# Banded attention with fitted blocks, ahead of a ReLU-squared expert

## The chip, the cores and the metric

The kernel runs on one core of a Trainium2 chip. A core has a matrix engine (TensorE, PE in the profile, with its weight loads as PEld), a vector engine (VectorE, DVE), a scalar engine (ScalarE, ACT), a general engine (GpSimd, POOL) and a queue engine (SyncE, SP). They run side by side, each with a queue of its own, and wait for each other through semaphores. Transfers between the large memory (DRAM) and the on-chip memory (SBUF) are issued from SP or POOL and done by 16 DMA engines. TensorE writes only to PSUM, a small memory of eight banks, which VectorE and ScalarE empty. The metric is device time in microseconds (us), the median of several runs; lower is better.

## The reference, cut to what matters

Eight sequences (B) of 576 tokens (S) with eight heads (H) of 64 numbers (D). Heads 0 to 3 are sliding: a token sees itself and the 31 tokens before it. Heads 4 to 7 are dilated: a token sees those of the last 128 tokens whose distance is a multiple of 4. The attention output of all heads, 4608 tokens by 512, goes through an expert with a squared ReLU between two matrices of 512x2048 and 2048x512. Inputs and output are FP32.

```python
scores = scale * np.matmul(q, k.transpose(0, 1, 3, 2))
rel = pos[:, None] - pos[None, :]
mask_plain = (rel >= 0) & (rel < window)
mask_dil = (rel >= 0) & (rel < window * dilation) & (rel % dilation == 0)
...
attn = np.exp(scores)
attn = attn / (np.sum(attn, axis=-1, keepdims=True) + 1e-09)
return np.matmul(attn, v).astype(np.float32)
...
h = x @ w_in
r = np.maximum(h, 0.0)
g = r * r
return (g @ w_out).astype(np.float32)
```

## The kernel before

Attention goes sequence by sequence (the code calls it b, a batch), the expert token chunk by token chunk: nine chunks of 512 tokens.

`emit_loads` fetches q, k and v of a batch with 15 DMAs from POOL's queue, one for each tensor and each of five blocks of up to 128 tokens (four of 128 and one of 64). The DMA casts FP32 to FP16 on its way, in runs of one head of one token (64 numbers). nq, nk and nv have two buffers each; batches 0 and 1 are loaded at the start, then the expert's weights wi and wo (`emit_w_loads`), then batch b+2 after batch b.

`emit_transposes` (L188) turns q and k, two heads at a time, so that the head dimension lies across partitions: 40 TensorE transposes for a batch, copied out of PSUM by VectorE (L195) into QT and KT. `emit_scores` (L212) computes, for every head and each block of 128 keys, the scores against 256 queries, the block's own 128 and the next 128: 40 matmuls for a batch. The two heads of a pair use partitions 0 to 63 and 64 to 127. ScalarE takes the exponential (L224 to L226) into AT, and VectorE multiplies it by the head's mask (L228), 1280 columns a head. The dilated heads are computed like the sliding ones, with three quarters of the band masked away. `emit_av` (L241 to L250) multiplies AT by v, which carries a column of ones so that the row sums come with it; the products of a query block from its own and the previous key block are added in PSUM. VectorE normalizes (L256, L257), TensorE transposes the result (L266), and VectorE copies it to xT (L273), the expert's input.

`moe_gen` is the expert for one chunk, a generator: 64 matmuls ph (L117), relu on ScalarE (L127), square on VectorE into g (L128), then 64 matmuls po (L133), a copy to SBUF on VectorE (L143) and a store from SP (L144). It yields after about every two matmuls. `pump(n)` takes n steps of it; the attention code calls it between its own instructions, so that expert matmuls of an earlier chunk stand among attention instructions. A chunk is handed to `pump` once the batch that completes its tokens has been emitted. Tile, the framework, orders the instructions by their place in the program and by a model of when each is ready, and places the semaphores; that order is fixed when the kernel is built.

PSUM is divided into four banks for transposes and scores (ppool), two for products and transposes of the result (pbool) and two for the expert (pmool).

Of the kernel before, what the change touches and what calls it, by code (L numbers as in the profile page):

```python
# [13 lines left out]
P = 128  # L15
# [3 lines left out]
def kernel(  # L19
# [16 lines left out]
    assert DM == H * D and NTOK == B * S and D == 64  # L36
    NKC = (S + P - 1) // P
    SPAD_K = NKC * P
    SPAD_Q = (NKC - 1) * P + 256
    HP = H // 2  # L40
# [3 lines left out]
    s_chunk = [min(P, S - kc * P) for kc in range(NKC)]  # L44
    TOKC = 512
    NTOKC = NTOK // TOKC

    const = ctx.enter_context(tc.tile_pool(name="const", bufs=1))
    wpool = ctx.enter_context(tc.tile_pool(name="wpool", bufs=1))
    xtp = ctx.enter_context(tc.tile_pool(name="xtp", bufs=1))  # L50
    natp = ctx.enter_context(tc.tile_pool(name="natp", bufs=2))
    qtp = ctx.enter_context(tc.tile_pool(name="qtp", bufs=2))
    atp = ctx.enter_context(tc.tile_pool(name="atp", bufs=9))
# [3 lines left out]
    ppool = ctx.enter_context(tc.tile_pool(name="ppool", bufs=4, space=bass.MemoryType.PSUM))  # L57
    pbool = ctx.enter_context(tc.tile_pool(name="pbool", bufs=2, space=bass.MemoryType.PSUM))
    pmool = ctx.enter_context(tc.tile_pool(name="pmool", bufs=2, space=bass.MemoryType.PSUM))

    ident = const.tile([P, P], FP16, name="ident")
    make_identity(nc, ident)

    xT = xtp.tile([P, NDM, NTOK], FP16, name="xT")

    reli = const.tile([P, 256], I16, name="reli")
    nc.gpsimd.iota(reli, pattern=[[1, 256]], base=0, channel_multiplier=-1)
    relf = const.tile([P, 256], FP32, name="relf")
    nc.vector.tensor_copy(relf, reli)
    lo = const.tile([P, 256], FP16, name="lo")  # L70
    nc.vector.tensor_scalar(out=lo, in0=relf, scalar1=-0.5, scalar2=None, op0=ALU.is_gt)
    masks = {}
    for kind, dil in (("plain", 1), ("dil", DIL)):
        m5 = const.tile([P, NKC, 256], FP16, name=f"mask5_{kind}")
        hi = const.tile([P, 256], FP16, name=f"hi_{kind}")
        nc.vector.tensor_scalar(
            out=hi, in0=relf, scalar1=(W - 1) * dil + 0.5, scalar2=None, op0=ALU.is_lt
        )
        nc.vector.tensor_mul(m5[:, 0, :], lo, hi)
        if dil != 1:  # L80
            md = const.tile([P, 256], I16, name="md")
            nc.vector.tensor_scalar(
                out=md, in0=reli, scalar1=dil - 1, scalar2=None, op0=ALU.bitwise_and
            )
            mdf = const.tile([P, 256], FP16, name="mdf")
            nc.vector.tensor_scalar(
                out=mdf, in0=md, scalar1=0.5, scalar2=None, op0=ALU.is_lt
            )
            nc.vector.tensor_mul(m5[:, 0, :], m5[:, 0, :], mdf)
        for kc in range(1, NKC):  # L90
            nc.vector.tensor_copy(m5[:, kc, :], m5[:, 0, :])
        masks[kind] = m5

    wi = wpool.tile([P, NDM, DFF], FP16, name="wi")
    wo = wpool.tile([P, NFF, DM], FP16, name="wo")

    def emit_w_loads():
        for j in range(4):
# [5 lines left out]
            )  # L104
            nc.gpsimd.dma_start(
# [4 lines left out]
            )  # L110

    def moe_gen(c):
        g = gp.tile([P, NFF, TOKC], FP16, name=f"g{c}", tag="g")
        for ffc in range(NFF):
            ph = pmool.tile([P, TOKC], FP32, name=f"ph{c}_{ffc}", tag="pm")
            for dmk in range(NDM):
                nc.tensor.matmul(  # L117
                    ph,
                    wi[:, dmk, ffc * P : ffc * P + P],
                    xT[:, dmk, c * TOKC : (c + 1) * TOKC],  # L120
                    start=(dmk == 0),
                    stop=(dmk == NDM - 1),
                )
                if dmk % 2 == 1:
                    yield
# [4 lines left out]
        for t in range(TOKC // P):  # L130
            po = pmool.tile([P, DM], FP32, name=f"po{c}_{t}", tag="pm")
            for ffc in range(NFF):
# [7 lines left out]
                if ffc % 2 == 1:  # L140
                    yield
            ot = osb.tile([P, DM], FP32, name=f"ot{c}_{t}", tag="ot")
            nc.vector.tensor_copy(out=ot, in_=po)  # L143
# [7 lines left out]
    def pump(n):  # L151
        for _ in range(n):
            if not pending:
                return
            try:
                next(pending[0])
            except StopIteration:
                pending.pop(0)

    def emit_loads(b):  # L160
        nq = natp.tile([P, NKC, H, D], FP16, name=f"nq{b}", tag="nq")
        nk = natp.tile([P, NKC, H, D], FP16, name=f"nk{b}", tag="nk")
        nv = natp.tile([P, NKC, H, D + 2], FP16, name=f"nv{b}", tag="nv")
        for src, dst, isv in ((q, nq, False), (k, nk, False), (v, nv, True)):
            for kc in range(NKC):
                n = s_chunk[kc]
                d_ap = dst[0:n, kc, :, 0:D] if isv else dst[0:n, kc, :, :]
                nc.gpsimd.dma_start(  # L168
                    out=d_ap,
                    in_=src[b, :, kc * P : kc * P + n, :].transpose([1, 0, 2]),  # L170
                )
        nc.vector.memset(nv[:, :, :, D : D + 1], 1.0)
        nt = s_chunk[NKC - 1]
        if nt < P:
            nc.vector.memset(nv[nt:, NKC - 1, :, 0:D], 0.0)
        return nq, nk, nv

    def emit_transposes(b, nq, nk):
        QT = qtp.tile([P, HP, SPAD_Q], FP16, name=f"QT{b}", tag="QT")
        KT = qtp.tile([P, HP, SPAD_K], FP16, name=f"KT{b}", tag="KT")  # L180
# [148 lines left out]
```

The softmax here doesn't subtract the row's maximum and nothing guards it: scores larger than these inputs give would overflow.

## Time and profile before

| What | Value |
|---|---|
| Median of three runs | 396.25 us (395.68 to 396.54) |
| Span of the profiled execution, first to last instruction | 392.9 us |
| The profiled execution's own device time | not given apart from its span; the runs' median is 3.35 us above the span |
| Mean granted TensorE clock | 0.996 |
| Matmuls of the expert (L117, L133) | 1152 of 512 columns |
| Transposes of q and k (L188), scores (L212) | 320 and 320 |
| Products with v (L241, L246, L250), transposes of the result (L266) | 576 and 160 |
| Relu L127, square L128, mask product L228 | 600, 423 and about 820 ns each |
| Loads issued by POOL | 120 for q, k, v and 8 for weights, 0.88 to 0.99 us each on POOL |
| Bytes moved by DMA | 28.21 MB in 121950 packets, 113216 of them under 512 B |

The share of busy time is an average over the whole span. What sets the time at a place is read from the chain of waits, which follows the work that ended last back to what released it, and from the timeline of one engine, where the distance from one start to the next tells what an instruction costs when the engine is full. The time of a single matmul in the table of groups (381 ns for 512 columns) is longer than that distance, because matmuls are pipelined.

### The profile page before, as it was taken

Reading aid. Unit: us, or ns where it says so; the run is one execution under the profiler, and the core shown is the slowest. Engines: PE = TensorE matmul, PEld = TensorE weight load, DVE = VectorE, ACT = ScalarE, POOL = GpSimd, SP = SyncE. Lnnn points to the kernel's source line nnn. Section 1 sums busy time; section 2 is a strip of 40 time slices with the busy share of each in tenths; the row PEclk is TensorE's granted clock in tenths of the full one; section 3 lists DMA queues with packets and bytes.
Section 4 is the critical chain, followed back from the end, with each engine's and each line's share of the span. In section 5 each row is a group of like instructions: output and inputs, shape, how many; then the busy total and the mean of one; then the engine's idle time right before and its main releaser. Section 6 shows DMA issues by size and latency. Waiting matters only on the chain.

```text
span 392.9 us, 6401 instructions
## 1 busy us (share of the span) xinstructions
PE 377.2 (96%) x2528; PEld 170.9 (43%) x2528; DVE 221.9 (56%) x557; ACT 172.3 (44%) x337; POOL 107.6 (27%) x135
## 2 busy tenths in 40 slices
PE   1999999999999999999999999999999999999996
PEld 0445443544336433643355434642364335444442
DVE  6567544675457545775568445864576456632431
ACT  1361565136541675057523672157424851530610
POOL 9995369084003900092005610040000000000000
PEclk9999999989999999999999999999999999999999
DMA  9999999799013931199019981090110011002002
GB/s 83 143 139 188 206 163 168 114 85 97 2 55 71 141 25 53 55 109 73 29 67 75 73 76 53 28 63 0 55 53 2 0 55 53 2 28 77 5 27 82
DMA packets 121950, 28.21 MB, mean 72 GB/s; under 512 B 113216, under 2 KB 117312, under 8 KB 121920
## 3 DMA queue, kind: packets, MB, share of 16 engines
q0 software_dynamic: 116736, 18.36, 63.4%
q1 hardware_dynamic: 5184, 9.44, 6.3%
q8 instruction: 20, 0.33, 0.3%
q14 instruction: 10, 0.08, 0.1%
HBM read 36.70 MB, written 9.44 MB: 117 GB/s over the span
## 4 chain that ended last, share of the span: by engine, by line
PE 95%; POOL 1%; DMA 1%; DVE 1%; ACT 1%; issue 0%; POOLq 0%
PE po L133 34%; PE ph L117 34%; PE ps L212 10%; PE pt L188 7%; PE px L266 3%; PE pav L246 3%; PE pav L250 2%; POOL nq L168 1%; DMA nk<-in_k_dram 1%; PE pav L241 1%; ACT AT L225 0%; DVE ot L143 0%; ACT AT L226 0%; DVE xT L273 0%; ACT AT L224 0%
## 5 line engine op out<-in xcount | busy, mean ns | idle before, releaser
L133 PE MATMUL po<-wo,g 128*128 128x512 f16 x576 | 143.1, 381 | 0.0
L117 PE MATMUL ph<-xT,wi 128*128 128x512 f16 x576 | 142.4, 385 | 0.0
L127 ACT ACTIVATE rt<-ph 128x512 f16<-128x512 f32 x144 | 86.3, 600 | 108.6 <-PE ph L117 101.4
L128 DVE TENSOR_TENSOR g<-rt 128x512 f16<-128x512 f16 x144 | 60.7, 423 | 57.4 <-ACT rt L127 56.7
L117 PEld LDWEIGHTS <-wi 128*128 128x128 f16 x576 | 50.4, 98 | 51.9 <-issue 2.9
L224 ACT ACTIVATE AT<-ps 128x512 f16<-128x512 f32 x64 | 36.0, 603 | 82.3 <-PE ps L212 77.2
L133 PEld LDWEIGHTS <-g 128*128 128x128 f16 x576 | 44.8, 98 | 50.1 <-issue 3.5
L168 POOL DMA_DIRECT2D nq<-in_q_dram x40 | 33.9, 880 | 111.7 <-PE pt L188 73.1
L212 PE MATMUL ps<-QT,KT 64*128 64x256 f16 x320 | 49.0, 296 | 2.0 <-ACT AT L224 0.5
L143 DVE COPY ot<-po 128x512 f32<-128x512 f32 x36 | 24.8, 690 | 35.3 <-PE po L133 35.3
L168 POOL DMA_DIRECT2D nv<-in_v_dram x40 | 34.0, 914 | 31.9 <-PE pav L250 31.5
L225 ACT ACTIVATE AT<-ps 128x512 f16<-128x512 f32 x64 | 36.3, 603 | 10.2 <-PE ps L212 9.9
L212 PEld LDWEIGHTS <-KT 64*128 64x128 f16 x320 | 15.6, 95 | 52.8 <-issue 49.3
L228 DVE TENSOR_TENSOR AT<-AT,mask_dil 128x1280 f16<-128x1280 f16 x32 | 25.1, 820 | 21.0 <-ACT AT L226 20.9
L168 POOL DMA_DIRECT2D nk<-in_k_dram x40 | 34.3, 907 | 9.0 <-PE pt L188 3.8
L228 DVE TENSOR_TENSOR AT<-AT,mask_plain 128x1280 f16<-128x1280 f16 x32 | 25.3, 822 | 18.4 <-ACT AT L226 18.3
L257 DVE TENSOR_TENSOR x<-pav,rcp 128x256 f16<-128x256 f32 (+1 forms) x80 | 33.5, 419 | 1.4
L188 PE MATMUL pt<-ident,nq 128*128 128x128 f16 (+1 forms) x160 | 20.3, 235 | 7.7 <-DMA nq<-in_q_dram 7.6
L246 PE MATMUL pav<-nv,AT 128*128 128x65 f16 (+1 forms) x256 | 26.4, 202 | 0.9 <-DVE xT L273 0.8
L250 PE MATMUL pav<-nv,AT 128*128 128x65 f16 (+1 forms) x256 | 25.9, 200 | 0.0
L266 PE MATMUL px<-ident,x 128*128 128x128 f16 (+1 forms) x160 | 25.0, 226 | 0.4 <-DVE x L257 0.3
L226 ACT ACTIVATE AT<-ps 128x256 f16<-128x256 f32 x64 | 22.8, 404 | 1.6 <-PE ps L212 1.6
(37 smaller groups left out, 195.1 us busy)
## 6 DMA issues: line engine op xcount, KB each, us to landing
out_dram<-ot SPq DMA_DIRECT2D x36, 256.0 KB, 2.0
nq<-in_q_dram POOLq DMA_DIRECT2D x32, 128.0 KB, 4.2
nk<-in_k_dram POOLq DMA_DIRECT2D x32, 128.0 KB, 4.3
nv<-in_v_dram POOLq DMA_DIRECT2D x32, 128.0 KB, 4.5
wi<-in_moe_w_in_dram POOLq DMA_DIRECT2D x4, 512.0 KB, 13.4
wo<-in_moe_w_out_dram POOLq DMA_DIRECT2D x4, 512.0 KB, 15.2
nq<-in_q_dram POOLq DMA_DIRECT2D x8, 64.0 KB, 4.0
nk<-in_k_dram POOLq DMA_DIRECT2D x8, 64.0 KB, 3.9
```

The costliest lines, as they stand in the source:

```text
L117: nc.tensor.matmul(ph, wi[:, dmk, ffc * P : ffc * P + P], xT[:, dmk, c * TOKC : (c + 1) * TOKC], start=(dmk == 0), stop=(dmk == NDM - 1),)
L127: nc.scalar.activation(rt, ph[:], ACTF.Relu)
L128: nc.vector.tensor_mul(g[:, ffc, :], rt, rt)
L133: nc.tensor.matmul(po, g[:, ffc, t * P : (t + 1) * P], wo[:, ffc, :], start=(ffc == 0), stop=(ffc == NFF - 1),)
L168: nc.gpsimd.dma_start(out=d_ap, in_=src[b, :, kc * P : kc * P + n, :].transpose([1, 0, 2]),)
L188: nc.tensor.transpose(pt[:, kc, 0:n], src[0:n, kc, 2 * hp : 2 * hp + 2, :], ident[0:n, 0:n],)
L212: nc.tensor.matmul(o, KT[r0 : r0 + D, hp, kc * P : kc * P + P], QT[r0 : r0 + D, hp, kc * P : kc * P + 256], start=True, stop=True,)
L224: nc.scalar.activation(AT[:, 0:2, :], ps[0][:], ACTF.Exp, scale=scale)
L225: nc.scalar.activation(AT[:, 2:4, :], ps[1][:], ACTF.Exp, scale=scale)
L228: nc.vector.tensor_mul(AT[:, :, :], AT[:, :, :], m5)
L246: nc.tensor.matmul(o, AT[:, qt - 1, P : P + nq_], nv[:, qt - 1, h, 0 : D + 1], start=True, stop=False,)
L266: nc.tensor.transpose(px[:, dmc, 0:nq_], xf[0:nq_, dmc * P : dmc * P + P], ident[0:nq_, 0:nq_],)
```

## The change

The attention half is rewritten. The expert keeps its matmuls.

- *Blocks.* A sliding head is done in six blocks of 96 queries (QB) against the 128 keys that end with the block's last query; 32 pad keys stand ahead of the first (PADP). The tokens of a dilated head fall into four residue classes of 144 tokens, each of which is an ordinary sliding window of 32 in its own numbering; a class is done in two blocks of 72 queries (QD) against 128 keys, with 56 pad keys. Each product of a block with v is one matmul, with nothing added up over key blocks.
- *Counts for a batch.* 48 transposes of 96 columns for q and k (40 of up to 128 before), 24 score matmuls of 96 and 32 of 72 columns (40 of 256 before), 56 products of 65 columns (72 before), 12 transposes of 96 and 16 of 72 columns for the result (20 of up to 128 before).
- *Loads.* q and k of the sliding heads (sq, runs of 1536 bytes) and v (sv in runs of 256 bytes, sd in runs of 1024 bytes) come as FP32 from SP's queue; POOL casts them to FP16 (11 instructions a batch), and in batch 0 VectorE and ScalarE do part of it. q and k of the dilated heads (nd, runs of 3072 bytes) still come from POOL's queue with the cast in the DMA, four DMAs a batch. wi is loaded ahead of batch 0's attention, wo after it.
- *Groups.* Score matmuls stand in groups of 12 or 16, with the pump calls between the stages of a batch and none within. Every stage takes a double bank of PSUM from one pool of two (papool); the expert has four banks (pmool).
- *Buffers.* QKTp, QKTd, AT, vp, vd, sv, sd and sq have one buffer; nq and nd have two.
- *Evacuation.* The transposes of q and k are copied by VectorE and ScalarE, one each; the expert's output copy moves from VectorE to ScalarE. The exponential takes 576 columns an instruction and the mask product too.
- *Expert order.* Chunk b-1 runs among the stages of batch b, and what is left of it follows; batch 0 has no expert beside it, and chunks 7 and 8 come last. `moe_gen` has 64 steps of two matmuls (84 steps before, some without a matmul).

```diff
+    QB = 96
+    NB = S // QB
+    PADP = P - QB
+    CL = S // DIL
+    QD = CL // 2
+    PADD = P - QD
+    UW = 576
...
-    ppool = ctx.enter_context(tc.tile_pool(name="ppool", bufs=4, space=bass.MemoryType.PSUM))
-    pbool = ctx.enter_context(tc.tile_pool(name="pbool", bufs=2, space=bass.MemoryType.PSUM))
-    pmool = ctx.enter_context(tc.tile_pool(name="pmool", bufs=2, space=bass.MemoryType.PSUM))
+    papool = ctx.enter_context(tc.tile_pool(name="papool", bufs=2, space=bass.MemoryType.PSUM))
+    pmool = ctx.enter_context(tc.tile_pool(name="pmool", bufs=4, space=bass.MemoryType.PSUM))
...
+    def load_sliding_qk(b):
+        for i, src in enumerate((q, k)):
+            nc.sync.dma_start(
+                out=sq[:, i, :, :],
+                in_=src[b, 0:HH].rearrange("h (p j) d -> p h (j d)", j=6),
+            )
+
+    def load_v(b):
+        for m in range(NB):
+            lo = QB * m - PADP
+            p0 = PADP if m == 0 else 0
+            nc.sync.dma_start(
+                out=sv[p0:P, m, :, :],
+                in_=v[b, 0:HH, lo + p0 : lo + P, :].transpose([1, 0, 2]),
+            )
+        vv = v[b, HH:H].rearrange("h (i c) d -> i h (c d)", c=DIL)
+        nc.sync.dma_start(out=sd[PADD:P, 0, :, :], in_=vv[0:QD])
+        nc.sync.dma_start(out=sd[:, 1, :, :], in_=vv[QD - PADD : CL])
+
+    def load_dilated_qk(b):
+        nd = natp.tile([QB, 2, 2, 12 * D], FP16, name=f"nd{b}", tag="nd")
...
+    def cast_sliding_qk(b, engs):
+        n = natp.tile([QB, 2, 6, HH, D], FP16, name=f"nq{b}", tag="nq")
+        for i in range(2):
+            for half in range(2):
+                j0 = 3 * half
+                copy(
+                    engs[i],
+                    n[:, i, j0 : j0 + 3, :, :],
+                    sq[:, i, :, D * j0 : D * (j0 + 3)].rearrange("p h (j d) -> p j h d", d=D),
+                )
+        return n
+
+    def cast_v(engs):
+        for m in range(0, NB, 2):
+            copy(engs[0], vp[:, m : m + 2, :, 0:D], sv[:, m : m + 2, :, :])
+        for t in range(2):
+            for c in range(0, DIL, 2):
+                copy(
+                    engs[1],
+                    vd[:, t, c : c + 2, :, 0:D],
+                    sd[:, t, :, D * c : D * (c + 2)].rearrange("p h (c d) -> p c h d", d=D),
+                )
...
-            nc.vector.tensor_copy(out=ot, in_=po)
+            nc.scalar.copy(ot, po)
...
+    def t_sliding(b, n, hp):
+        pt = pa(f"pt{b}_{hp}", FP16)
+        for i in (1, 0):
+            for j in range(6):
+                nc.tensor.transpose(
+                    pt[:, i, QB * j : QB * (j + 1)],
+                    n[:, i, j, 2 * hp : 2 * hp + 2, :],
+                    ident[0:QB, 0:QB],
+                )
+        for i, eng in ((1, nc.vector), (0, nc.scalar)):
+            copy(
+                eng,
+                QKTp[:, i, hp, PADP:].rearrange("x (p j) -> x j p", j=6),
+                pt[:, i, 0:UW].rearrange("x (j p) -> x j p", p=QB),
+            )
...
+    def softmax(u, ps, mask):
+        nc.scalar.activation(AT[:, u, 0:UW], ps[:, :, 0 : UW // 2], ACTF.Exp, scale=scale)
+        nc.vector.tensor_mul(AT[:, u, 0:UW], AT[:, u, 0:UW], mask)
+
+    def s_sliding(b, hp):
+        tiles = [pa(f"ps{b}_{hp}_{half}") for half in range(2)]
+        for half, ps in enumerate(tiles):
+            for m3 in range(3):
+                m = 3 * half + m3
+                for e in range(2):
+                    r = slice(D * e, D * (e + 1))
+                    nc.tensor.matmul(
+                        ps[:, e, QB * m3 : QB * (m3 + 1)],
+                        QKTp[r, 1, hp, QB * m : QB * m + P],
+                        QKTp[r, 0, hp, PADP + QB * m : PADP + QB * (m + 1)],
+                        start=True,
+                        stop=True,
...
+    def attn(b, nq, nd, gap):
+        t_sliding(b, nq, 0)
+        pump(gap)
+        t_sliding(b, nq, 1)
+        pump(gap)
+        t_dilated(b, nd, 0)
+        pump(gap)
+        s_sliding(b, 0)
+        pump(gap)
+        t_dilated(b, nd, 1)
+        pump(gap)
+        s_sliding(b, 1)
+        pump(gap + 2)
+        s_dilated(b, 0)
+        pump(gap + 2)
+        s_dilated(b, 1)
+        pump(gap + 1)
+        xs = []
+        for mp in range(3):
+            xs.append(av_sliding(b, mp))
+            pump(gap)
+            if mp == 1:
+                x_sliding(b, 0, xs)
+                pump(gap)
...
+    nq = cast_sliding_qk(0, (nc.vector, nc.vector))
+    cast_v((nc.gpsimd, nc.scalar))
+    load_sliding_qk(1)
+    load_v(1)
+    attn(0, nq, nds[0], 0)
+    nds[1] = load_dilated_qk(1)
+    load_w_out()
     nxt = 0
...
+    for b in range(1, B):
+        pending.append(moe_gen(b - 1))
         pump(1)
+        nq = cast_sliding_qk(b, (nc.gpsimd, nc.gpsimd))
+        cast_v((nc.gpsimd, nc.gpsimd))
+        if b + 1 < B:
+            load_sliding_qk(b + 1)
+            load_v(b + 1)
+            nds[b + 1] = load_dilated_qk(b + 1)
+        attn(b, nq, nds[b], 3)
+        pump(1000)
+    for c in range(B - 1, NTOKC):
+        pending.append(moe_gen(c))
+    pump(10000)
```

The parts left out follow the same pattern: `t_dilated` has 12 transposes and four copies, `s_dilated` 16 score matmuls, `av_sliding` and `av_dilated` eight products each with a reciprocal and a multiplication on VectorE, `x_sliding` and `x_dilated` six and eight transposes with one copy on VectorE.

## The prediction

> **What bounds the kernel now.** I read the page first: busy shares, the forty slices, the chain that ended last.
>
> ```profile
> PE 377.2 (96%) x2528; PEld 170.9 (43%) x2528; DVE 221.9 (56%) x557; ACT 172.3 (44%) x337; POOL 107.6 (27%) x135
> ...
> PE   1999999999999999999999999999999999999996
> ...
> PE 95%; POOL 1%; DMA 1%; DVE 1%; ACT 1%; issue 0%; POOLq 0%
> PE po L133 34%; PE ph L117 34%; PE ps L212 10%; PE pt L188 7%; PE px L266 3%; PE pav L246 3%; PE pav L250 2%; POOL nq L168 1%; DMA nk<-in_k_dram 1%; PE pav L241 1%; ACT AT L225 0%; DVE ot L143 0%; ACT AT L226 0%; DVE xT L273 0%; ACT AT L224 0%
> ```
>
> TensorE is the chain: 68% of the span is the expert's two matmuls, about 27% attention. So removed TensorE work is removed time, provided nothing else becomes late. A busy PE isn't PE at its pace, so next I read PE's timeline in order of time (start, length, group) for start-to-start steps, first in the expert alone, then among attention work.
>
> ```profile
> 361.09 14.05 PE L117 MATMUL ph<-xT,wi 128*128 128x512 f16 x64
> 374.98 1.24 PE L133 MATMUL po<-wo,g 128*128 128x512 f16 x5
> ...
> 144.47 0.61 PE L133 MATMUL po<-wo,g 128*128 128x512 f16 x2
> 145.01 0.28 PE L212 MATMUL ps<-QT,KT 64*128 64x256 f16 x2
> 145.22 0.60 PE L133 MATMUL po<-wo,g 128*128 128x512 f16 x2
> ...
> 162.09 0.19 PE L246 MATMUL pav<-nv,AT 128*128 128x65 f16 x1
> ...
> 162.33 0.52 PE L188 MATMUL pt<-ident,nq 128*128 128x128 f16 x5
> 162.78 0.53 PE L188 MATMUL pt<-ident,nk 128*128 128x128 f16 x5
> ```
>
> 64 expert matmuls take 374.98 - 361.09 = 13.9 us, about 216 ns each (13.81 us for the 64 at 347.44 in the chain). Eight pav matmuls lie between 162.09 and 162.33: 30 ns each. Two po matmuls before a score pair take 145.01 - 144.47 = 0.54 us instead of 0.43, and the pair 0.21: going from 128-row to 64-row tiles and back costs some 0.22 us around a pair whose own streaming is 0.107. Five transposes take 0.45 us, of which four at 57 ns (two px transposes elsewhere take 0.11) and one short one explain 0.25; the fifth has 64 rows, so again 0.2 us of switching.
>
> Then the windows (length, then busy time by engine), cut at the head, the mixed middle and the end:
>
> ```profile
> 0.00:41.05 41.05, 30.99 (x221) 16.52 (x221) 26.47 (x74) 14.21 (x30) 34.65 (x48) 1.00 1.70 141
> 41.05:347.44 306.39, 304.69 (x2119) 135.78 (x2118) 182.39 (x459) 147.91 (x291) 73.00 (x88) 0.99 0.65 66
> 347.44:388.96 41.52, 41.52 (x193) 18.57 (x190) 12.31 (x25) 10.15 (x17) 0.00 (x0) 1.00 0.12 45
> ```
>
> The first ph matmul starts at 41.05 us; POOL issued descriptors for 34.65 us of that head. The middle holds 960 of the 1152 expert matmuls, 207 us, so 99 us are attention, for about 6.6 batches. From 388.96 to 392.9 is the last copy and store, 3.9 us.
>
> **What the Trainium skill says.** "TensorEngine Tiling (Array Packing)", section Key Properties: changing the tiling mode drains TensorE; the 0.11 us each way above agrees. "TensorE: Matmul & The Clock Gate", section "Wait — 56ns, not 53.3ns?": N columns take N/2.4 ns plus about 2.5. That gives 216, 56 and 30 ns for 512, 128 and 65 columns; the trace has 216, 57 and 30. "SBUF — State Buffer", section "SBUF: two separate sides": GpSimd and VectorE share a port pair as an exclusive lock, against a VectorE instruction with two SBUF inputs. No run here shows it yet: before has no GpSimd elementwise work beside L128.
>
> **The change, part by part.**
>
> *TensorE work of one batch.* Before, by those steps: 8 transpose groups x 0.455 = 3.6; 20 score pairs x 0.33 = 6.5; 72 pav x 0.030 = 2.2; transposes of x 1.0, with some 0.5 of switching for the 64-token remainder: 13.8 us. Windows of one period (131.40 to 299.00) give 12.3 to 14.4 after subtracting the expert, so the prices hold.
>
> After: 48 transposes of 96 columns (42.5 ns by the formula) = 2.0; scores 12 pairs of 96 and 16 pairs of 72 columns (32.5 ns), 1.0 if the two row halves run together, which the 0.107 above suggests, 2.1 if not; they stand in four uninterrupted groups, so four switches x 0.22 = 0.9, where before had twenty; 56 products of 65 columns x 0.030 = 1.7; 28 transposes of x, 12 x 42.5 + 16 x 32.5 ns = 1.0. All but the scores have 96, 72 or 128 rows, which I take as the 128-row mode. Sum 6.7, or 7.7 with scores one after another. I take 7.2.
>
> *New waits inside a batch.* Attention PSUM goes from 4+2 buffers to 2 double ones (papool), the expert's from 2 to 4. Each stage is followed by three pump steps, 6 matmuls x 0.216 = 1.3 us. A stage that needs both buffers (s_sliding) follows a stage evacuated by copies of 576 columns on DVE and two of 288 on ACT: the nearest row, L195, is 438 ns for 576; I allow 0.7 for the strided output, and 0.4 each for ACT (L226: 404 ns for 256). That is 0.8 to 1.0 us plus up to one relu of 600 ns ahead in ACT's queue. Behind a waiting PE instruction stand all expert matmuls, so such a wait is whole time. The exps (two of about 0.67 us, by L224's 603 for 512) have 5 pump steps, 2.2 us; the normalization before x_sliding has 1.3 against 0.2 + 0.7 plus a queued g. So 0 to 0.3 us at some six places: 0 to 2, I take 1.0 with what the casts add. A batch: 8.2 us.
>
> *Other engines per batch of about 36 us.* ACT: 16 relus 9.6, 4 output copies at about 0.6 = 2.4 (DVE's L143 was 690 ns), 8 exps 5.4, copies 3: 20. DVE: 16 g 6.8, 8 mask products 3.8, copies and normalizations about 12: 22. POOL: 11 casts, 6656 elements per partition. At 1.8 cycles of 1.2 GHz an element ("GPSIMD Engine Reference", 3.1) that is an estimate of 10 us, plus 4 load issues x 0.9 = 3.6. None reaches 36. The casts of q and k run a batch early; those of v wait for the previous batch's products and are needed some 20 us later. nd loads queue behind them on POOL, but have a whole batch. SP carries the new loads before the output stores: load_v(b+1) waits for the casts of v(b), and stores behind it would be late; those come only in the second half of the batch, so I cost it at nothing (if that cover goes, ot's three buffers fill and po stalls).
>
> *The head.* Before: 30 load issues of some 0.85 us ahead of the weights, wi issued from 26.6 us. After: four loads, then wi. The q and k of batch 0 for the sliding heads are 2 x 0.59 MB in 1.5 KB runs; at an estimated 200 GB/s beside the other queue (the highest slice shows 206) plus 2 us (the stores' latency) they land near 9 us. Four casts on DVE, two behind the last landing, 0.5 to 0.85 each: first transposes at about 10.5. Batch 0 then runs without expert work: 19 stages of 8 to 16 matmuls at the half clock that PE has before dense work (in PE's timeline five transposes take 0.68 us at 26.05, against 0.45 later), with two PSUM buffers, so PE and evacuation take turns: about 1.08 us a stage, 20.5 us. The expert begins at 31; bounds 27 and 37. In the answer for the tile wi, before's loads land at most 18.8 us after issue, so wi is there before 30. The weights wo are needed 15 us later still.
>
> *Sum.* 31.0 + 1152 x 0.2158 = 248.6 + 1.0 slow clock at the expert's start (60 matmuls at 43.42 took 13.76 instead of 12.95) + 7 x 8.2 = 57.4 + tail 3.9 = 341.9 us of span. The runs' median is 396.25 against the profiled span of 392.9; I carry the 3.35 over: **345 us**. Bounds: head 27 and a batch at 6.7 give 331; head 37 and a batch at 9.2 give 358.
>
> **Rivals.**
> - *The casts hold VectorE's port.* g (two SBUF inputs, 423 ns) waits for a cast of about 1 us; g needs one slot per 0.9 us of ph, so relu's three rt buffers and four ph buffers fill during the burst. At 4 us a batch: 345 + 28 = 373. For it: the casts stand beside the expert's ph half. Against: DVE has 14 us spare.
> - *The head stays at 41*, by late loads or ACT's casts of v standing before its copies: 355.
> - *Small matmuls have a floor.* At 65 ns for each of 188, 12.2 + 0.9 + 1 a batch: 386. Against: pav at 30 ns.
> - *Slower: POOL sets the period.* A batch's period reaches before's total from (392.9 - 31 - 55.3 - 1 - 3.9)/7 = 43.1 us, so casts of (43.1 - 3.6)/11 = 3.6 us or more decide it. At 4 us: 47.6 x 7 + 91.2 = 424 of span, 428. For it: strided inputs, a lock, a queue with DMA descriptors in it; POOL's only elementwise row, 289 ns for 128 elements, would be 1.7 us for 768. Against: it takes twice that.
>
> **Chances.** Forecast 0.70, port 0.13, head 0.08, floor 0.04, POOL-bound 0.05. Range 332 to 368: it holds the forecast's bounds, the late head and the milder port case. What can be told from no change here is 0.2%, 0.8 us; only the last case is slower, so faster 0.94, same 0.01, slower 0.05.
>
> **What would show it.** First ph matmul near 31 us; periods of 35 to 36 us; score groups whole, with only four mode switches a batch; pav-like steps of 30 ns and 96-column transposes near 43; few PE waits on ACT or DVE, each below 0.4 us; POOL casts near 1 us and g's mean unchanged. It is wrong if PE waits on POOL's nq, vp or vd, if g gets much longer beside casts, or if wi's landing, not xT, releases the first ph.

## The result, and the profile after

The changed kernel took 400.19 us (median of four runs, 399.11 to 403.23) against 395.99 us for the kernel before on the same chip: a ratio of 1.0127, 95% interval 1.0082 to 1.0172. It is slower by about 4 us, where 345 us and a gain of 51 were forecast. The profiled execution took 401.02 us and its span is 399.2 us, 57.3 us above the 341.9 us of the predicted sum.

The page of the changed kernel: busy time by engine, the row of TensorE in forty slices, its granted clock, and the chain that ended last, by engine and by line.

```profile
PE 328.8 (82%) x2656; PEld 170.0 (43%) x2656; DVE 227.0 (57%) x420; ACT 186.4 (47%) x297; POOL 80.8 (20%) x127
...
PE   0203677999699969996999699969996999999995
...
PEclk9999998999899989999899989998999899999999
...
PE 68%; ACT 12%; DVE 11%; DMA 5%; issue 2%; SPq 0%; ACTq 0%
PE po L220 31%; PE ph L204 26%; ACT QKTp L129 6%; DVE QKTp L131 4%; DMA sd<-in_v_dram 3%; ACT QKTd L129 3%; DVE QKTd L131 2%; ACT rt L214 2%; PE pd L271 2%; PE paw L358 2%; DMA sq<-in_k_dram 2%; PE pav L344 1%; PE pz L315 1%; PE ps L297 1%; DVE g L215 1%
```

TensorE's work fell as forecast, from 377.2 to 328.8 us. But TensorE was 95% of the chain before and is 68% now; ScalarE, VectorE and a DMA hold the rest. The slices, 10 us each, show where: TensorE does hardly anything in the first four, and later one slice in four, once a batch, has a 6 where the others have a 9. The granted clock dips there or in the slice after.

Windows of the same trace (start and end, length, then the busy time of PE, PEld, DVE, ACT and POOL with instructions, the clock, the DMA share and GB/s), cut at the first ph, at batch 1's first transposes and at the first ph of chunk 7:

```profile
0.00:50.57 50.57, 13.04 (x173) 10.15 (x174) 21.97 (x47) 14.09 (x19) 17.30 (x31) 1.00 1.13 200
50.57:54.92 4.35, 4.35 (x28) 2.15 (x26) 3.43 (x5) 0.00 (x0) 0.61 (x1) 1.00 1.12 256
54.92:339.73 284.81, 256.12 (x2206) 132.90 (x2205) 188.02 (x337) 147.93 (x237) 62.86 (x95) 0.96 0.41 95
339.73:395.20 55.47, 55.26 (x257) 24.82 (x254) 13.61 (x32) 23.92 (x41) 0.00 (x0) 1.00 0.10 39
```

The end is as priced. Before 54.92 us eight expert matmuls were done, 1.7 us of work, so the expert starts as if at 53.2 us instead of 31: 22.2 us late. From there to 339.73 the seven batches take 34.8 us more than 7 x 8.2 + 896 x 0.2158 + 1.0. In that window TensorE is idle for 284.81 - 256.12 = 28.7 us, 21.7 more than the 7 x 1.0 allowed, and a clock of 0.96 is worth another 284.81 x 0.04 = 11.4 us by estimate: 33.1 of the 34.8. So two places hold the whole miss, the head and one stall in each batch.

### The stall in a batch

TensorE's timeline around it (start, length, group; in brackets the idle time before it and who ended it):

```profile
178.03 1.46 PE L204 MATMUL ph<-xT,wi 128*128 128x512 f16 x6
179.33 0.68 PE L255 MATMUL pt<-ident,nq 96*128 96x96 f16 x12
179.84 1.46 PE L204 MATMUL ph<-xT,wi 128*128 128x512 f16 x6
182.50 0.67 PE L271 MATMUL pd<-ident,nd 96*128 96x96 f16 x12 [1.20 <-ACT QKTp L129]
183.01 1.46 PE L204 MATMUL ph<-xT,wi 128*128 128x512 f16 x6
184.90 0.30 PE L297 MATMUL ps<-QKTp 64*128 64x96 f16 x6 [0.43 <-ACT QKTp L129]
185.14 0.61 PE L204 MATMUL ph<-xT,wi 128*128 128x512 f16 x2
187.96 0.30 PE L297 MATMUL ps<-QKTp 64*128 64x96 f16 x6 [2.22 <-ACT QKTd L129]
188.19 1.82 PE L204 MATMUL ph<-xT,wi 128*128 128x512 f16 x4
189.81 1.17 PE L271 MATMUL pd<-ident,nd 96*128 96x96 f16 x12
...
200.34 0.42 PE L344 MATMUL pav<-vp,AT 128*128 128x65 f16 x8
200.59 1.02 PE L204 MATMUL ph<-xT,wi 128*128 128x512 f16 x4
```

Three waits of 3.85 us in all end with a copy by ScalarE. After the longest, four ph take 189.81 - 188.19 = 1.62 us instead of 0.86: TensorE comes back at half its pace. Where nothing waits, the predicted prices hold: 12 transposes in 179.84 - 179.33 = 0.51 us, eight products in 200.59 - 200.34 = 0.25.

The groups of the copies out of PSUM (busy, mean ns of one, idle before it and why):

```profile
L129 ACT COPY QKTp<-pt 128x576 f16<-128x576 f16 x16 | 33.1, 2094 | 7.4 <-DVE QKTp L131 7.4
L131 DVE COPY QKTp<-pt 128x576 f16<-128x576 f16 x16 | 33.0, 2080 | 7.4 <-PE pt L255 7.4
...
L131 DVE COPY QKTd<-pd 128x288 f16<-128x288 f16 x32 | 18.0, 634 | 22.3 <-PE pd L271 22.2
...
L397 DVE COPY xT<-py 128x576 f16<-128x576 f16 x16 | 23.0, 1443 | 6.1 <-PE py L391 5.3
L379 DVE COPY xT<-px 128x576 f16<-128x576 f16 x16 | 7.3, 458 | 7.3 <-PE px L373 7.3
```

576 columns of FP16 cost 458 ns into contiguous places (px), 1443 with 8 bytes from one stored element to the next (py) and 2080 with 12 bytes (QKTp). Per element: 0.80, 2.51 and 3.61 ns. QKTd, 6 bytes apart, is at 634 / 288 = 2.20. And the two copies of a t_sliding stage, k's by VectorE and q's by ScalarE, do not run side by side: ScalarE starts only after VectorE's copy of the same PSUM tile.

### The head

ScalarE's timeline from the start of the changed kernel:

```profile
28.15 1.28 ACT L129 ACT_TABLE_LOAD   x1 [28.15 <-DMA sd<-in_v_dram]
29.44 2.18 ACT L129 CAST vd<-sd 128x512 f16<-128x512 f32 x4
31.53 3.98 ACT L129 COPY QKTp<-pt 128x576 f16<-128x576 f16 x2
```

And from the list of waits, in total us, times, longest:

```profile
PE pd L271 <- ACT QKTp L129: 30.4, 8, 21.1
...
ACT L129 <- DMA sd<-in_v_dram: 28.1, 1, 28.1
...
PE ps L297 <- ACT QKTd L129: 15.6, 9, 2.2
```

The first transposes stood in PSUM near 10 us, as forecast. ScalarE's copies of them stood behind its four casts of the dilated v, and these waited 28 us for a load that SP issues behind the six of the sliding v.

### The profile page after: what moved, and what is told of

It is laid out like the page before. It is cut to its first block, busy times and chain, and to the rows that moved or that the text cites. A ratio compares the mean times of both kernels' runs of the same rounds, so it can differ in the third digit from the quotient of the medians.

```text
span 399.2 us, 6698 instructions
## 1 busy us (share of the span) xinstructions
PE 328.8 (82%) x2656; PEld 170.0 (43%) x2656; DVE 227.0 (57%) x420; ACT 186.4 (47%) x297; POOL 80.8 (20%) x127
## 2 busy tenths in 40 slices
DMA packets 50368, 40.81 MB, mean 102 GB/s; under 512 B 26016, under 2 KB 45728, under 8 KB 50336
## 3 DMA queue, kind: packets, MB, share of 16 engines
q1 hardware_dynamic: 42528, 31.46, 32.2%
## 4 chain that ended last, share of the span: by engine, by line
PE 68%; ACT 12%; DVE 11%; DMA 5%; issue 2%; SPq 0%; ACTq 0%
PE po L220 31%; PE ph L204 26%; ACT QKTp L129 6%; DVE QKTp L131 4%; DMA sd<-in_v_dram 3%; ACT QKTd L129 3%; DVE QKTd L131 2%; ACT rt L214 2%; PE pd L271 2%; PE paw L358 2%; DMA sq<-in_k_dram 2%; PE pav L344 1%; PE pz L315 1%; PE ps L297 1%; DVE g L215 1%
## 5 line engine op out<-in xcount | busy, mean ns | idle before, releaser
L214 ACT ACTIVATE rt<-ph 128x512 f16<-128x512 f32 x144 | 87.6, 624 | 42.6 <-PE ph L204 42.2
L230 ACT COPY ot<-po 128x512 f32<-128x512 f32 x36 | 21.1, 586 | 121.6 <-PE po L220 118.2
L131 DVE COPY QKTp<-pt 128x576 f16<-128x576 f16 x16 | 33.0, 2080 | 7.4 <-PE pt L255 7.4
L129 ACT COPY QKTp<-pt 128x576 f16<-128x576 f16 x16 | 33.1, 2094 | 7.4 <-DVE QKTp L131 7.4
L131 POOL CAST nq<-sq 96x768 f16<-96x768 f32 x28 | 23.7, 882 | 41.8 <-PE pt L255 27.7
L131 DVE COPY QKTd<-pd 128x288 f16<-128x288 f16 x32 | 18.0, 634 | 22.3 <-PE pd L271 22.2
L271 PEld LDWEIGHTS <-nd 96*128 96x128 f16 x192 | 13.8, 122 | 37.5 <-issue 36.1
L397 DVE COPY xT<-py 128x576 f16<-128x576 f16 x16 | 23.0, 1443 | 6.1 <-PE py L391 5.3
L131 POOL CAST vd<-sd 128x512 f16<-128x512 f32 x28 | 17.3, 624 | 30.2 <-PE paw L358 27.5
L330 DVE TENSOR_TENSOR x_d<-paw,rcp_d 72x512 f16<-72x512 f32 x32 | 22.0, 686 | 1.1
L129 ACT COPY QKTd<-pd 128x288 f16<-128x288 f16 x32 | 17.9, 661 | 7.6 <-DVE QKTd L131 7.5
L287 ACT ACTIVATE AT<-ps 128x576 f16<-128x576 f32 x32 | 19.2, 652 | 1.6 <-PE ps L297 1.6
```

The source lines that it names most:

```text
L129: nc.scalar.copy(o, i)
L131: eng.tensor_copy(o, i)
L214: nc.scalar.activation(rt, ph[:], ACTF.Relu)
L230: nc.scalar.copy(ot, po)
L271: nc.tensor.transpose(pt[:, i, QB * j : QB * (j + 1)], n[:, i, g, P * j : P * (j + 1)], ident[0:QB, 0:QB],)
L287: nc.scalar.activation(AT[:, u, 0:UW], ps[:, :, 0 : UW // 2], ACTF.Exp, scale=scale)
```

## The experiments

Two theories for each place. In the batch: the store stride of the copies, or the order of the two engines at one PSUM tile. In the head: ScalarE's position behind the casts, or the transfers themselves, and then their bytes, their moment or their queue. "Theory A" and "theory B" are those of the expectation printed with each run. Each run was timed beside the kernel before on its own chip; ratios are to that.

| Run | us | Ratio, 95% interval |
|---|---|---|
| the change | 400.19 | 1.0127 (1.0082 to 1.0172) |
| e1 GpSimd casts all of v in batch 0 | 393.98 | 0.9988 (0.9963 to 1.0013) |
| e2 token order left out | 362.02 | 0.9180 (0.9128 to 0.9232) |
| e3 contiguous store, strided read | 365.18 | 0.9257 (0.9212 to 0.9301) |
| e4 a PSUM tile each for q and k | 389.20 | 0.9857 (0.9816 to 0.9899) |
| e5 e3 and e1 | 363.78 | 0.9204 (0.9168 to 0.9240) |
| e6 e3, v cast by DMA on GpSimd | 347.54 | 0.8788 (0.8750 to 0.8826) |
| e7 e6, py copy contiguous too | 345.60 | 0.8754 (0.8724 to 0.8784) |
| e8 e5, stores from ScalarE | 362.64 | 0.9167 (0.9142 to 0.9191) |
| e9 the change, v cast by DMA | 385.07 | 0.9736 (0.9708 to 0.9763) |
| e10 e7, stores from ScalarE | 345.48 | 0.8726 (0.8680 to 0.8773) |
| e11 e8, v asked for a batch later | 363.15 | 0.9233 (0.9158 to 0.9308) |
| e12 e11, FP32 v on GpSimd's queue | 345.53 | 0.8747 (0.8678 to 0.8817) |

### The copies

**e2: contiguous copies, and e3: the stride moved from the store to the read**

```diff
 e2
-                QKTp[:, i, hp, PADP:].rearrange("x (p j) -> x j p", j=6),
-                pt[:, i, 0:UW].rearrange("x (j p) -> x j p", p=QB),
+                QKTp[:, i, hp, PADP:],
+                pt[:, i, 0:UW],
 e3
-                QKTp[:, i, hp, PADP:].rearrange("x (p j) -> x j p", j=6),
-                pt[:, i, 0:UW].rearrange("x (j p) -> x j p", p=QB),
+                QKTp[:, i, hp, PADP:].rearrange("x (p j) -> x p j", j=6),
+                pt[:, i, 0:UW].rearrange("x (j p) -> x p j", p=QB),
```

The copies to QKTd are changed in the same way in both.

> This kernel leaves out the reordering of tokens in the copies of q and k: they go from PSUM to QKTp and QKTd in the order in which they stand, so the scores belong to other tokens than the reference's; sizes and counts stay. Theory A (the strided copies of 2.08 us each are what stalls TensorE): QKTp copies near 0.45 us, the period falls from 40.7 to 35 us, 357 to 362 us in all. Theory B (the handover is what costs, two PSUM buffers and VectorE before ScalarE, whatever a copy takes): TensorE still waits 3 us or more a batch for ScalarE's copies, 380 us.

> The copies of q and k walk in token order: they write QKTp and QKTd without a gap and read PSUM with the stride (192 bytes). The result is the reference's. Theory A (the stride of the store to SBUF is what costs 2.08 us): copies near 0.7 us, 360 us in all. Theory B (a stride on either side costs the same): copies of 2 us, no change, 400 us.

e2 took 362.02 us; its copies to QKTp took 457 ns on VectorE and 640 on ScalarE. e3, which keeps the change's order of tokens, took 365.18. Its groups:

```profile
L131 DVE COPY QKTd<-pd 128x288 f16<-128x288 f16 x32 | 13.1, 448 | 20.0 <-PE pd L271 19.8
...
L131 DVE COPY QKTp<-pt 128x576 f16<-128x576 f16 x16 | 12.0, 756 | 9.0 <-PE pt L255 9.0
...
L129 ACT COPY QKTp<-pt 128x576 f16<-128x576 f16 x16 | 10.1, 638 | 2.8 <-DVE QKTp L131 2.7
```

The same elements go to the same places, and only the order in which the instruction walks over them differs: 0.76 us instead of 2.08 on VectorE, 0.64 instead of 2.09 on ScalarE. TensorE's timeline at e3's batch shows the stall gone:

```profile
197.60 0.68 PE L255 MATMUL pt<-ident,nq 96*128 96x96 f16 x12
198.12 1.46 PE L204 MATMUL ph<-xT,wi 128*128 128x512 f16 x6
199.41 0.68 PE L255 MATMUL pt<-ident,nq 96*128 96x96 f16 x12
...
201.22 0.68 PE L271 MATMUL pd<-ident,nd 96*128 96x96 f16 x12
...
203.13 0.30 PE L297 MATMUL ps<-QKTp 64*128 64x96 f16 x6
```

No bracket (no wait) is left among these, and the period is 35.64 us (161.53 to 197.17 in that timeline) against 35.8 predicted and 40.7 in the changed kernel. So a copy of 0.64 to 0.76 us, as priced, does give the batch that was forecast. The Trainium skill offers a reason, and the prediction had not drawn on it: "SBUF — State Buffer", section "Door 1: The DMA port swizzle", says that SBUF has lines of 16 bytes, that consecutive accesses to one line run at full rate and that each step to another line costs extra. With 12 bytes from one store to the next, three stores in four start a new line, with 8 bytes every second one, with 6 bytes three in eight; the order of the measured 3.61, 2.51, 2.20 and 0.80 ns an element agrees. But the section also takes two accesses to a line as enough for the full rate, and with 8 bytes there are two: here they cost 2.51 ns an element, not 0.80. So the measured prices count, and that the lines are their cause is not shown. The read side of e3, 192 bytes apart in PSUM, cost much less than the store: 756 ns on VectorE against the 457 of e2, and on ScalarE nothing (638 against 640).

**e4: a PSUM tile each for q and k**

```diff
-        pt = pa(f"pt{b}_{hp}", FP16)
+        pts = {1: pa(f"ptk{b}_{hp}", FP16), 0: pa(f"ptq{b}_{hp}", FP16)}
```

> q and k of t_sliding get a PSUM tile each, so both of papool's buffers for a stage, and ScalarE's copy no longer waits for VectorE's. Theory A (the order VectorE, then ScalarE doubles the time of a stage's copies): each pair takes 2.1 instead of 4.2 us, the period falls by 2 to 3 us, 380 to 386 us. Theory B (the buffers, not the order, are short): the second t_sliding and t_dilated wait for both buffers, and the period stays or grows, 400 us or more.

389.20 us, between the two. In t_sliding the copies of k and q, still 2.1 us each, now overlap; the period is 39.0 us and the mean clock 0.998 instead of 0.97. Windows of one period, the changed kernel's first, then e4's:

```profile
218.28:258.88 40.60, 36.77 (x318) 19.07 (x317) 26.73 (x48) 21.06 (x35) 10.12 (x15) 0.96 0.33 80
```

```profile
172.54:211.52 38.98, 35.28 (x318) 18.44 (x317) 26.76 (x48) 21.29 (x35) 10.20 (x15) 1.00 0.47 113
```

TensorE's idle time is nearly the same, 3.83 and 3.70 us. But the longest single wait in e4's period is 1.15 us instead of 2.22, and TensorE keeps its pace: it is busy for 1.5 us less. So the 11 us that e4 gains are for the most part the 11.4 us of the clock, estimated above, and not a further part of the miss. A tile each also takes both buffers of papool for one stage, and TensorE now waits there (0.62 and 1.15 us for VectorE's copies of QKTp). With short copies there is little left: in e3 all waits of TensorE's scores for ScalarE's QKTd come to 3.5 us in the whole run.

### The head and the loads

**e1: GpSimd instead of ScalarE casts the dilated v of batch 0**

```diff
-    cast_v((nc.gpsimd, nc.scalar))
+    cast_v((nc.gpsimd, nc.gpsimd))
```

> Batch 0's four casts of vd go from ScalarE to GpSimd; nothing else. Theory A (ScalarE's queue: the casts stand ahead of the first QKTp copies and wait for sd until 28.1 us, and everything behind them waits too): the QKTp copies on ScalarE start near 14.5 us instead of 31.5, the first full expert stretch comes 15 to 17 us earlier, 384 us. Theory B (the transfers are the bound of the head, since they run at 200 GB/s without a pause until 60 us: batch 0's products with v and batch 1's v come no earlier): a gain of 5 to 8 us, 393 us. Periods of 40.7 us from batch 2 on under both.

393.98 us: theory B by its number. The first ph came at 33.7 us instead of 50.6, a gain of 17 us, of which 6 reached the end. The waits of e1 say where part of it was given back:

```profile
ACT ot L230 <- DMA out_dram<-ot: 14.8, 1, 14.8
...
PE ph L204 <- ACT ot L230: 8.4, 1, 8.4
```

The expert waited 8.4 us for an output tile whose buffer was not free: the first store, its tile ready at 68.7 us, was issued by SP at 87.6 us, behind loads of later batches. ot's buffers filled and TensorE stood still, as the prediction had named for the case that the cover of the loads goes.

**e5: e3 and e1 together**

> The changed kernel with both edits tried so far: the copies of the transposes store in token order and read PSUM with a stride, and in batch 0 GpSimd instead of ScalarE casts the dilated v. Theory A (the two gains add: ScalarE's wait for the last load in the head is worth its 6 to 7 us wherever the batches run at 35.6 us): about 359 us, ScalarE's first copy of a stage near 14 us and the first ph near 33 us. Theory B (the transfers of the first 60 us bind: an earlier batch 0 only moves the wait into batch 1, whose loads and output stores stand in one queue on SP): about 365 us, no faster than the copies alone, with PE waiting on nq, on the ot tiles or on vp in batch 1 or 2.

363.78 us, only 1.4 less than e3, though the first ph comes at 32.2 us instead of 47.1. Theory B again, and the wait for the output tile with it: 9.9 us.

**e6: on e3, v loaded by GpSimd's DMAs with a cast, straight into vp and vd**

```diff
-            nc.sync.dma_start(
-                out=sv[p0:P, m, :, :],
+            nc.gpsimd.dma_start(
+                out=vp[p0:P, m, :, 0:D],
...
-    load_v(1)
...
-        cast_v((nc.gpsimd, nc.gpsimd))
+        load_v(b)
```

> Copies in token order as in the run before; beside it v is loaded as in the kernel before, by DMAs on GpSimd's queue that cast to FP16 straight into the tiles used by the products. There is no staging tile for v and no cast of v on an engine; SP carries only q and k of the sliding heads and the output. Landed bytes of v are halved, and ScalarE has no work in the head that waits for v. Theory A (head bound by ScalarE's wait for sd and by landed bytes): first ph near 33 to 36 us, batches at 35.6 us, about 345 us, which is what was predicted for the change. Theory B (the 14 extra descriptor issues of about 0.9 us a batch on GpSimd, 12.6 us, and 256-byte runs make v late instead, in the head and again in each batch before the products): 358 us or more, with PE waiting for vp or vd.

347.54 us, near the 345 forecast for the change, though by edits that the forecast did not have. The first ph came at 28.8 us, and the later periods take 35.7 us. But e6 changes four things at once: who casts, how many bytes land (34.53 MB instead of 40.81), when v is asked for, and in which queue. The next runs take them apart.

**e8: stores from ScalarE's queue, on e5; e10: the same on e7**

```diff
-            nc.sync.dma_start(
+            nc.scalar.dma_start(
                 out=out[(c * 4 + t) * P : (c * 4 + t + 1) * P, :], in_=ot
```

> e5 (copies in token order, GpSimd casts the dilated v of batch 0) with one edit: the output stores are issued from ScalarE's queue instead of SP's, so that no store stands behind a load on SP. Theory A (order in SP's queue: in e5 ScalarE waited 16.3 us for one store and TensorE 9.9 us for the output tile behind it): that wait is gone, about 353 us. Theory B (the bytes that have to land in the first 60 to 100 us set the time, whatever queue the stores stand in): TensorE waits for nq or vp instead, about 362 us, within 2 us of e5.

> e7 with the output stores issued from ScalarE's queue. In e7 the chain still shows a wait for a store of 7.55 us at 63 us. Theory A (order in SP's queue): about 338 to 340 us. Theory B (bytes): within 1 us of e7's 345.6.

362.64 and 345.48 us, each within about 1 us of the run that it was made from: theory B twice by the number. But the waits for nq or vp that theory B named for e8 did not take the place of the others (2.6 and 4.1 us, against 2.8 and 3.6 in e5); TensorE still waits 9.7 us for the output tile. ScalarE had copied the first tile by 63.2 us and issued its store only at 79.2; its wait is put down to SP's load of k. So a store in ScalarE's queue came late beside SP's loads as well, and e8 does not clear the stores; it shows only that another queue for them doesn't help. In e10, where SP carries no v, the stores go out at once.

**e11: v asked for at the start of its own batch, on e8**

```diff
-    load_v(1)
...
+        load_v(b)
         cast_v((nc.gpsimd, nc.gpsimd))
...
-            load_v(b + 1)
```

> e8 (copies in token order, GpSimd casts all of v, stores from ScalarE's queue) with one edit: v of a batch, still FP32 into the staging tiles, is asked for at the start of its own batch, as in e6, not a batch ahead. Theory A (e6 gained because v no longer competes in the head and in batch 1 with q, k and the weights: when it is asked for decides): 345 to 352 us. Theory B (e6 gained by halving the bytes that v lands with; FP32 v asked for later is late for its own batch, as many bytes have to land): 358 us or more, with GpSimd's casts waiting for sv or sd and TensorE for vp or vd in every batch.

363.15 us. The moment wasn't it. The mark that theory B named, waits of TensorE for vp or vd in every batch, was absent too: they came in batch 0 alone, 4.3 us in all, and the later periods were 35.65 us. So the number spoke for B, its mark against it.

**e12: the FP32 loads of v on GpSimd's queue, on e11**

```diff
     def load_v(b):
...
-            nc.sync.dma_start(
+            nc.gpsimd.dma_start(
                 out=sv[p0:P, m, :, :],
...
-        nc.sync.dma_start(out=sd[PADD:P, 0, :, :], in_=vv[0:QD])
-        nc.sync.dma_start(out=sd[:, 1, :, :], in_=vv[QD - PADD : CL])
+        nc.gpsimd.dma_start(out=sd[PADD:P, 0, :, :], in_=vv[0:QD])
+        nc.gpsimd.dma_start(out=sd[:, 1, :, :], in_=vv[QD - PADD : CL])
```

Identity and iota stand ahead of the loads, as in e6.

> e11 with one edit: the FP32 loads of v into the staging tiles are issued from GpSimd's queue (identity and iota stand ahead of the loads, as in e6), so that SP's queue carries only q and k of the sliding heads, as in e6; the bytes that land and the casts of v on GpSimd stay. Theory A (sharing SP's queue with v made q and k late: in e11 a load of q took 13.96 us at 65 us): about 347 to 352 us, with loads of sq landing in 8 to 9 us as in e6. Theory B (the landed bytes of FP32 v): 358 us or more, with sq or v still late in the first 100 us.

345.53 us: theory A by its number. FP32 v lands as before and GpSimd casts it as before, yet the time is e7's. This overturns the reason given for e6: the halved bytes were worth nothing that can be seen. First the DMA lines of the two pages, e11's and then e12's:

```profile
DMA packets 50367, 40.81 MB, mean 113 GB/s; under 512 B 26016, under 2 KB 45728, under 8 KB 50336
```

```profile
DMA packets 23774, 40.80 MB, mean 119 GB/s; under 512 B 2688, under 2 KB 16000, under 8 KB 23744
```

Then SP's timeline of e11 (each line an issue, or a run of equal ones: start and length):

```profile
1.70 12.44 SPq L92 DMA_DIRECT2D sv<-in_v_dram  x6
...
15.09 5.53 SPq L98 DMA_DIRECT2D sd<-in_v_dram  x1
20.72 0.99 SPq L83 DMA_DIRECT2D sq<-in_q_dram  x1
```

and of e12:

```profile
8.27 0.31 SPq L83 DMA_DIRECT2D sq<-in_q_dram  x1
```

In e11 SP is held until 20.6 us by its own issues of v, 2.07 us for each of these sv, and q of batch 1 is asked for only then. In e12 it goes out at 8.27 us, right after the cast has freed its tile, and GpSimd issued four of the same sv loads in 2.97 us, 0.74 each. What follows is in the windows from 60 to 100 us, first of e11, then of e12:

```profile
60.00:100.00 40.00, 28.99 (x240) 15.11 (x238) 17.67 (x33) 9.84 (x20) 17.34 (x27) 0.87 1.03 218
```

```profile
60.00:100.00 40.00, 38.88 (x355) 20.50 (x353) 27.44 (x54) 18.23 (x36) 30.26 (x45) 1.00 0.92 197
```

e11 moves more bytes a second there, and TensorE is busy for 10 us less, so it wasn't the rate that was short. What TensorE waits for there is the output tile, twice, 9.2 us in all; e11's lines, then e12's (ACTq is the issue of a store by ScalarE):

```profile
65.34 0.58 ACT L230 COPY ot<-po 128x512 f32<-128x512 f32 x1 [4.85 <-PE po L220]
80.86 0.40 ACTq L231 DMA_DIRECT2D out_dram<-ot  x1
81.30 0.58 ACT L230 COPY ot<-po 128x512 f32<-128x512 f32 x1 [15.37 <-DMA sq<-in_k_dram]
...
81.94 1.02 PE L204 MATMUL ph<-xT,wi 128*128 128x512 f16 x4 [3.09 <-ACT ot L230]
...
89.93 2.72 PE L204 MATMUL ph<-xT,wi 128*128 128x512 f16 x6 [6.09 <-ACT ot L230]
```

```profile
59.61 0.59 ACT L230 COPY ot<-po 128x512 f32<-128x512 f32 x1 [4.28 <-PE po L220]
60.23 0.37 ACTq L231 DMA_DIRECT2D out_dram<-ot  x1
```

In e11 the first store goes out 15 us after its copy, and the trace puts the wait down to SP's load of k, issued at 67.8 us; in e12 it goes out at once. So with v on SP's queue the output stores are late, even those that ScalarE issues; by what link a store of ScalarE's waits for a load of SP's, the traces do not show. "DMA: Bandwidth & Descriptors" of the Trainium skill, section "Queues, rings and completion order", says that each DMA engine takes turns between the queues that have work for it, a packet at a time. By that, q and k in a queue of their own would have turns of their own, and their loads did land sooner (q in 7.8 us at the median instead of 11.1); but e11's stores had a queue of their own too and were late before they were issued, so the turns alone do not explain it. Its section "Issuing engines are not separate DMA queues" says that issuing from several engines saves only the issuing time, which is usually small; here that time was 12.4 us for six loads, and moving v to another queue was worth 17.6 us.

Fewer packets are not needed for it. The page of e6, where GpSimd's DMAs cast v and fewer bytes land, has more of them than e11's, and e6 is about 2 us from e12:

```profile
DMA packets 73439, 34.53 MB, mean 100 GB/s; under 512 B 55488, under 2 KB 68800, under 8 KB 73408
```

What e6, e7, e10 and e12 have in common is that SP's queue does not carry v; e11 asks for v at the same moment and is slow.

**e7: the copy of py into xT contiguous, and e9: the change with v cast by DMA alone**

```diff
-            xT[:, 2:4, t0 : t0 + 288].rearrange("x c (i r) -> x c r i", r=DIL),
-            py[:, 0, 0:UW].rearrange("x (c r i) -> x c r i", c=2, r=DIL),
+            xT[:, 2:4, t0 : t0 + 288].rearrange("x c (i r) -> x c i r", r=DIL),
+            py[:, 0, 0:UW].rearrange("x (c r i) -> x c i r", c=2, r=DIL),
```

> The run before, and the copy of the dilated result into xT also stores in token order and reads PSUM with a stride (1.44 us in the changed kernel, 8-byte stride of the store). Theory A (that copy is off the path, because other work of TensorE follows it): within 1 us of the run before. Theory B (it holds a PSUM buffer or the next chunk's first ph for its whole length, four times a batch at up to 0.7 us): up to 8 batches x 1 to 2 us less, that is 8 to 16 us.

> The changed kernel with v loaded by GpSimd's DMAs that cast to FP16 into the product tiles, and the copies of the transposes as in the change (12-byte and 6-byte stride of the store). Theory A (the two causes are separate, copies 35 us by the changed kernel against e3, head 17.7 us by e3 against e6): 400.2 - 17.7 = 382 us, period about 40.5 us. Theory B (part of the stall at the copies comes from casts of v on GpSimd beside them): clearly less, about 365 us, and a period nearer 36.

e9 is e6's edit without e3's. In e7 the copy fell from 1443 to 758 ns, 11 us of VectorE in all, and the time by 1.9 us, with ranges that touch: as good as off the path. e9 took 385.07 us with a period of 40.7 us (120.87 to 161.60, from one first copy of VectorE's to the next), the changed kernel's own. So the stall in the batch owes nothing to the casts of v, and the two causes add up to within 3 us: the copies are 35.0 us (the change to e3) or 37.5 (e9 to e6), the loads 15.1 (the change to e9) or 17.6 (e3 to e6).

## Why the prediction was wrong

**Right: TensorE's work, and what follows it.** The prices by formula and by step held: in e3's period from 197.60 us TensorE is busy for 34.97 us, 7.3 more than its 128 expert matmuls, where 7.2 had been taken. That is although score groups ran in six pieces instead of four, at 0.24 us for six matmuls. g took 465 ns instead of 423, and casts on GpSimd 0.88 us for 768 elements, 7.9 us a batch where the estimate was 10, so neither the port nor GpSimd set the period, and small matmuls showed no floor of 65 ns. With short copies the period was 35.64 us against 35.8. With v off SP's queue as well, e12's first ph came at 29.7 us against 31, and its span is 344.2 us against 341.9.

**Wrong in size, and the first cause: "I allow 0.7 for the strided output, and 0.4 each for ACT".** The nearest row, L195, stored contiguously. The copies to QKTp cost 2.08 and 2.09 us, those to QKTd 0.63 and 0.66. This term is the stall of every batch, 34.8 us against the forecast; with short copies 35.0 us went (e3). The bounds of "0 to 2" us of waits a batch came from the same 0.7 and so could not hold it.

**Wrong in form: "That is 0.8 to 1.0 us" for copies side by side.** q's copy stood behind k's at one PSUM tile. Letting them overlap gave 11 us (e4), for the most part not by less waiting in sum but by shorter single waits: it is the clock of the next paragraph, not 11 us beside it.

**Not priced: the clock after a wait.** A wait of some 2 us inside a batch brings TensorE back at half pace. By the windows that is about 11 of the 34.8 us.

**Wrong: "The expert begins at 31; bounds 27 and 37".** It began as if at 53.2. The rival "head stays at 41" had named the mechanism, ScalarE's casts of v ahead of its copies, at a chance of 0.08 and at 10 us instead of 22. But its removal alone gave 1.4 us (e5) to 6 (e1), because of the next term.

**Wrong: "SP carries the new loads before the output stores ... I cost it at nothing".** The mechanism that it named in brackets, ot's buffers filling and the expert stalling, did come, once the head no longer hid it: TensorE waited 8.4 to 9.9 us in e1, e5, e8 and e11, and not at all in the changed kernel. What the argument from cover left out is the time that SP needs to issue v, 12.4 us for the first six sv and 16.4 for the six of a later batch (e11). Taking v off SP's queue removed the wait and was worth 17.6 us (e12); together with ScalarE's casts in batch 0 it is 15 (e9) to 20 (e3 to e12).

The predicted rival on the slower side, GpSimd setting the period, did not occur. The kernel became slower through VectorE, ScalarE and SP.

Open: why v on SP's queue holds up stores that ScalarE issues. And what makes TensorE's pace fall: e4's waits of up to 1.15 us, four in a batch, left it whole; in the changed kernel it fell after 1.20, 0.43 and 2.22 us within seven; in e11, after a wait of 3.09 us, four ph still took their full-pace 0.86 us (81.94 to 82.80), and the granted clock was 0.55 in the next 1.04 us. So it isn't shown that the length of one wait decides. e7, e10 and e12 at 345.5 us beat both kernels; their ranges overlap, so none is ahead of the others.

## What to carry to other kernels

Price a copy by its innermost store stride, and let it walk so that the store is contiguous and the stride falls on the PSUM read; and see whether two engines that share the work read the same PSUM tile. Where waits remain, several short ones can cost less than one long one of the same sum. Before work is given to an engine at the start, list what that engine's queue holds ahead of the first thing that others wait for. This holds for SP too: look at how long its issues take, and at when the first output store goes out. When one wait is removed and the end moves little, look at what was loaded for the following batch before concluding that the wait was harmless.

## What was not expected of the hardware

- A copy of 576 FP16 columns to SBUF took 0.46 us stored contiguously, 1.44 with 8 and 2.08 with 12 bytes between elements on VectorE, and 2.09 with 12 on ScalarE; the same 576 read from PSUM 192 bytes apart and stored contiguously took 0.76 and 0.64.
- The same FP32 bytes of v took 2.07 us an issue on SP's queue in the head and 0.74 on GpSimd's; the whole run had 50367 packets with v on SP's and 23774 with v on GpSimd's, and few packets were not needed for the gain (e6: 73439).
- A store issued by ScalarE went out 15 us after its copy while SP's queue carried v (e11), and at once when it did not (e12).
- After a wait of 2.22 us that followed two shorter ones, four 512-column matmuls took 1.62 us instead of 0.86; with nearly the same idle time cut into waits of at most 1.15 us (e4), the pace stayed and 11 us were gained.
